# Weight conversion from 64-bit floats: two VectorE bit instructions and a product with zero in place of three VectorE instructions and a maximum

## The chip, the cores and the metric

The kernel runs on one core of a Trainium2 chip. The core has a matrix engine (TensorE, PE in the rows; PEld is its weight load), VectorE (DVE), ScalarE (ACT), GpSimd (POOL), SyncE (SP, which here only issues transfers) and 16 DMA engines. Each engine works through its own queue in order and waits for the others by semaphores. The metric is the device time of one execution, in microseconds; smaller is better.

## The reference

Three stages follow each other: attention inside chunks of 64 tokens, a channel mix with a squared ReLU and a sigmoid gate, and a top-2 mixture of four causal attention experts. What matters here is the second stage and the type of its weights:

```python
'w_k': np.random.randn(d_model, d_ff).astype(np.float32) * (1.0 / np.sqrt(d_model))
...
def _moe_ref(x, mu_k, mu_r, w_k, w_v, w_r) -> np.ndarray:
    x_prev = np.concatenate([np.zeros((B, 1, D), dtype=np.float32), x[:, :-1, :]], axis=1)
    xk = mu_k * x + (1.0 - mu_k) * x_prev
    xr = mu_r * x + (1.0 - mu_r) * x_prev
    k = np.maximum(xk @ w_k, 0.0)
    v = k * k @ w_v
    r = 1.0 / (1.0 + np.exp(-(xr @ w_r)))
    return (r * v).astype(np.float32)
```

The factor `1.0 / np.sqrt(...)` is a 64-bit float, so `w_k` (512 x 1024), `w_v` (1024 x 512) and `w_r` (512 x 512) arrive as 64-bit floats. The kernel reads them as pairs of 32-bit words and makes 32-bit floats of them itself.

## The kernel before, in words

`attn_mix` does the first two stages together. Tokens come in units of 384, twelve in all. For a unit, the attention steps (`s_T`, `s_S`, `s_PV`, `s_PT`) load queries, keys and values, transpose them on TensorE (line 148, result `Tps`), make scores (`Sps`, lines 182 and 185), a softmax on VectorE and ScalarE (lines 190 to 199) and the product with the values (`PVps`, lines 216 and 219), copied by ScalarE to `XT` (line 44). `s_shift` mixes each token with the one before it (lines 274 to 279, results `xhr`, `xlr`, `xhk`, `xlk`: a high and a low part each). Then come the products `mps` of the channel mix, on lines 57 to 59: three matmuls for each pair of blocks, high with high, low with high and high with low. So each weight is needed as a high part and a low part as well (`wrh`, `wrl`, `wkh`, `wkl`, `wvh`, `wvl`).

The weights are made by `conv` in 20 chunks of 128 x 512: 4 of `w_r`, 8 of `w_k`, 8 of `w_v`, in that order. A chunk's 512 KB are loaded into a tile `st` (line 340); `h` is every second word of it (sign, exponent and top of the mantissa), `l` the words between. ScalarE writes |h|, read as a 32-bit float, to the tile `cz` (line 346). POOL raises it to at least 2^-15 (line 347), so that a zero stays within the range that the bits can say. Three VectorE instructions then build the 32-bit float: shift left by 3 and mask (line 348), put in the top three bits of `l` (line 349), put in the sign of `h` (line 350). `split` makes the high part on POOL (line 46) and the low part on VectorE (line 360).

Two `st` buffers and two `cz` buffers go round (the first four chunks use other tiles for `st`). So the load of a chunk waits until line 350 of the chunk two before it is through; and it waits on SP's queue, ahead of the loads of queries, keys and values issued later.

Some 12 chunks are converted while the first attention tiles are made, by the order in `CFG["pro"]`; the others while the first unit's products run (`convert` in the last loop of `attn_mix`). In each engine's queue the instructions stand in an order that a planner made out of this program order, from its own idea of how long each takes; the trace shows attention and conversion interleaved one by one. After the twelve units come the experts, lines 485 to 901.

Of the kernel before, what the change touches and what calls it, by code (L numbers as in the profile page):

```python
# [11 lines left out]
ACTF = mybir.ActivationFunctionType  # L12
ALU = mybir.AluOpType
# [2 lines left out]
DRAM = bass.MemoryType.DRAM  # L16


F64_ZERO = 2.0 ** -15

CH = 64
UNIT = 384
# [26 lines left out]
def f32(ap):  # L49
    return ap.bitcast(F32)  # L50
# [11 lines left out]
def attn_mix(tc, at, x2T, q, k, v, mu_k, mu_r, w_k, w_v, w_r, ident, attended_all, mixed_k):  # L62

    nc = tc.nc
# [10 lines left out]
    scale = 1.0 / float(D) ** 0.5  # L75

    with ExitStack() as ctx:
# [254 lines left out]
        def conv(src, dst, g, c0, n):  # L332

            i = done[0] - 1
            if i < 4:

                st = wkr.tile([128, n, 2], I32, tag=("xhr", "xlr", "xhk", "xlk")[i], name="st")
            else:
                st = at.tile([128, n, 2], I32, tag="st", bufs=CFG["stb"], name="st")
            nc.sync.dma_start(out=st.rearrange("p f w -> p (f w)"),  # L340
                              in_=src.bitcast(I32)[g * 128:(g + 1) * 128, 2 * c0:2 * (c0 + n)])
            h, l = st[:, :, 1], st[:, :, 0]
            z = at.tile([128, n], F32, tag="cz", bufs=2, name="cz")
            b = z.bitcast(I32)

            nc.scalar.activation(out=z, in_=f32(h), func=ACTF.Abs)
            nc.gpsimd.tensor_scalar(z, z, F64_ZERO, None, op0=ALU.max)
            nc.vector.tensor_scalar(b, b, 3, 0x3FFFFFF8, op0=ALU.logical_shift_left, op1=ALU.bitwise_and)
            nc.vector.scalar_tensor_tensor(b, l, 29, b, op0=ALU.logical_shift_right, op1=ALU.bitwise_or)
            nc.vector.scalar_tensor_tensor(b, h, -(1 << 30), b, op0=ALU.bitwise_and, op1=ALU.bitwise_or)  # L350
            split(z, dst, g, c0, n)

        def conv32(src, dst, g, c0, n):
# [4 lines left out]
        def split(z, dst, g, c0, n):  # L358
            copy(nc, CFG["chi"], dst.hi[:, g, c0:c0 + n], z)
            eng(nc, nth(CFG["clo"], done[0])).tensor_tensor(dst.lo[:, g, c0:c0 + n], z, f32(dst.hi[:, g, c0:c0 + n]), op=ALU.subtract)  # L360
# [593 lines left out]
```

## Time and profile before

| | us |
|---|---|
| median of 3 runs | 1010.99 (1010.32 to 1011.34) |
| the profiled execution, its own time | 1009.65 |
| its span, first to last instruction | 1007.8 |
| PE busy | 950.1 (94%) |
| DVE busy | 682.0 (68%) |
| ACT busy | 547.2 (54%) |
| POOL busy | 396.4 (39%) |

The profiled execution took 1.34 us less than the median, and 1.85 us of it lie outside its span. Busy time is summed over the span; which engine limits a stretch is read from the busy time of that stretch and from the waits in it.

### The profile page before, as it was taken

Reading aid. Unit: us, or ns where it says so; the run is one execution under the profiler, and the core shown is the slowest. Engines: PE = TensorE matmul, PEld = TensorE weight load, DVE = VectorE, ACT = ScalarE, POOL = GpSimd, SP = SyncE. Lnnn points to the kernel's source line nnn. Section 1 sums busy time; section 2 is a strip of 40 time slices with the busy share of each in tenths; the row PEclk is TensorE's granted clock in tenths of the full one; section 3 lists DMA queues with packets and bytes.
Section 4 is the critical chain, followed back from the end, with each engine's and each line's share of the span. In section 5 each row is a group of like instructions: output and inputs, shape, how many; then the busy total and the mean of one; then the engine's idle time right before and its main releaser. Section 6 shows DMA issues by size and latency. Waiting matters only on the chain.

```text
span 1007.8 us, 21843 instructions
## 1 busy us (share of the span) xinstructions
PE 950.1 (94%) x8038; PEld 909.6 (90%) x8038; DVE 682.0 (68%) x1690; ACT 547.2 (54%) x1271; POOL 396.4 (39%) x519
## 2 busy tenths in 40 slices
PE   3679899998999999999999999999999999999997
PEld 2569899998999899999999999989899999989985
DVE  5899936557654766775667432587776867877895
ACT  3478564535343534444454413476666857676674
POOL 5444402636453645455454536413331232233101
PEclk8789999999999999999999999999999999999999
DMA  9784342253425352524223124674553547263412
GB/s 228 191 213 130 96 98 79 48 126 64 106 36 115 63 123 53 126 41 104 54 53 84 32 64 117 119 185 115 131 136 99 174 83 201 66 179 93 141 44 96
DMA packets 218979, 108.42 MB, mean 108 GB/s; under 512 B 182920, under 2 KB 195320, under 8 KB 218872
## 3 DMA queue, kind: packets, MB, share of 16 engines
q1 hardware_dynamic: 188600, 67.16, 29.2%
q0 software_dynamic: 30272, 39.86, 14.5%
q8 instruction: 64, 1.05, 0.5%
q14 instruction: 43, 0.35, 0.1%
HBM read 66.01 MB, written 28.38 MB: 94 GB/s over the span
## 4 chain that ended last, share of the span: by engine, by line
PE 53%; DVE 7%; ACT 2%; DMA 2%; issue 1%; POOL 0%; DVEq 0%; SPq 0%; ACTq 0%; POOLq 0%
PE mps L57 8%; PE mps L58 8%; PE mps L59 8%; PE pj L57 6%; PE pj L59 6%; PE pj L58 6%; PE Sps L657 4%; PE Tps L717 3%; PE AVps L750 2%; PE AVps L746 2%; DVE PTl L724 1%; DVE sm L659 1%; DMA x<-x2T 1%; ACT P L669 1%; DVE Q L554 1%
## 5 line engine op out<-in xcount | busy, mean ns | idle before, releaser
L57 PE MATMUL mps<-xhk,wkh 128*128 128x384 f32 x384 | 131.7, 344 | 4.6 <-DVE r L305 4.3
L58 PE MATMUL mps<-xlk,wkh 128*128 128x384 f32 x384 | 129.1, 337 | 0.0
L59 PE MATMUL mps<-xhk,wkl 128*128 128x384 f32 x384 | 128.9, 336 | 0.0
L57 PE MATMUL mps<-kh,wvh 128*128 128x384 f32 x384 | 128.0, 340 | 0.9 <-DVE r L305 0.9
L59 PE MATMUL mps<-kh,wvl 128*128 128x384 f32 x384 | 127.3, 335 | 0.9 <-DVE wvl L360 0.9
L58 PE MATMUL mps<-kl,wvh 128*128 128x384 f32 x384 | 128.0, 335 | 0.0
L309 POOL TENSOR_TENSOR kl<-r,kh 128x384 fp32r<-128x384 f32 x80 | 87.2, 1091 | 69.7 <-ACT kh L308 69.5
L305 DVE TENSOR_TENSOR r<-mps,r 128x384 f32<-128x384 f32 x80 | 44.4, 555 | 95.0 <-ACT r L302 83.3
L669 ACT ACTIVATE P<-sm,nm 128x512 f32<-128x512 f32 (+3 forms) x144 | 83.9, 584 | 24.0 <-DVE nm L659 19.9
L659 DVE CUSTOM_DVE_ANT_0 sm<-Sps,mask 128x256 f32<-128x256 f32 (+4 forms) x160 | 74.3, 477 | 22.4 <-PE Sps L657 21.2
L263 POOL TENSOR_TENSOR xa<-XT 128x384 f32<-128x384 f32 x72 | 67.6, 947 | 53.4 <-DVE xlr L279 27.6
L766 POOL TENSOR_TENSOR Yf<-Yf,zb 128x576 f32<-128x576 f32 x14 | 20.0, 1428 | 153.6 <-DVE Yf L761 153.3
L57 PEld LDWEIGHTS mps<-xhk,wkh 128*128 128x128 f32 x384 | 72.2, 188 | 6.9 <-DVE r L305 5.5
L308 ACT ACTIVATE kh<-r 128x384 fp32r<-128x384 f32 x96 | 50.7, 528 | 46.0 <-DVE r L305 45.1
L724 DVE TENSOR_TENSOR PTl<-Tps,PTh 128x512 fp32r<-128x512 f32 (+2 forms) x144 | 70.7, 504 | 6.9 <-ACT PTh L723 5.6
L57 PEld LDWEIGHTS mps<-kh,wvh 128*128 128x128 f32 x384 | 71.9, 188 | 1.9 <-DVE r L305 1.2
L59 PEld LDWEIGHTS mps<-kh,wvl 128*128 128x128 f32 x384 | 71.8, 188 | 1.2 <-DVE wvl L360 1.2
L58 PEld LDWEIGHTS mps<-xlk,wkh 128*128 128x128 f32 x384 | 72.3, 188 | 0.1
L59 PEld LDWEIGHTS mps<-xhk,wkl 128*128 128x128 f32 x384 | 72.2, 188 | 0.0
L58 PEld LDWEIGHTS mps<-kl,wvh 128*128 128x128 f32 x384 | 72.1, 188 | 0.1
L57 PE MATMUL mps<-xhr,wrh 128*128 128x384 f32 x192 | 66.5, 348 | 4.7 <-ACT sig L292 3.8
L277 DVE SCALAR_TENSOR_TENSOR xa<-xa,mu,XT 128x384 f32<-128x384 f32 x72 | 63.4, 893 | 10.8 <-POOL xa L263 10.8
(192 smaller groups left out, 2761.5 us busy)
## 6 DMA issues: line engine op xcount, KB each, us to landing
x2T<-x2d POOLq DMA_DIRECT2D x48, 384.0 KB, 3.4
x<-x2T POOLq DMA_DIRECT2D x32, 576.0 KB, 5.7
K<-Kph SPq DMA_DIRECT2D x64, 128.0 KB
out_dram<-o SPq DMA_DIRECT2D x32, 256.0 KB
ldq<-in_q_dram SPq DMA_DIRECT2D x176, 32.0 KB
ldk<-in_k_dram SPq DMA_DIRECT2D x176, 32.0 KB
ldv<-in_v_dram SPq DMA_DIRECT2D x20, 256.0 KB
st<-in_moe_w_k_dram SPq DMA_DIRECT2D x8, 512.0 KB
```

The lines of the kernel that those rows point to most:

```text
L57: nc.tensor.matmul(out=out, lhsT=ah, rhs=bh, start=first and i == 0, stop=False)
L58: nc.tensor.matmul(out=out, lhsT=ah, rhs=bl, start=False, stop=False)
L59: nc.tensor.matmul(out=out, lhsT=al, rhs=bh, start=False, stop=last and i == n - 1)
L263: nc.gpsimd.tensor_tensor(d, now, prev, op=ALU.subtract)
L277: nc.vector.scalar_tensor_tensor(a, d, m, prev, op0=ALU.mult, op1=ALU.add)
L305: nc.vector.tensor_tensor(r2, p, r, op=ALU.mult)
L308: nc.scalar.activation(out=o.hi, in_=r2, func=ACTF.Copy)
L309: eng(nc, CFG["klo"][u >= CFG["nearly"]]).tensor_tensor(o.lo, r2, f32(o.hi), op=ALU.subtract)
L657: issued = nc.tensor.matmul(out=pp[:, :w], lhsT=x, rhs=y[:, a:a + w], start=n == 0, stop=n == len(terms) - 1)
L659: nc.vector.tensor_tensor_reduce(out=sm[:, a:a + w], in0=pp[:, :w], in1=mk[:, :w], op0=ALU.add, op1=ALU.min, scale=-scale, scalar=3e38, ac ...
L669: nc.scalar.activation(out=x[:, :nk], in_=sm[:, :nk], func=ACTF.Exp, scale=-1.0, bias=nm[:, :1], accum_out=z)
L724: nc.vector.tensor_tensor(l, src, f32(h), op=ALU.subtract)
```

## The change

ScalarE no longer writes |h| but h times 2^-112, sign and all, which takes the difference of the two exponent offsets away. POOL no longer works on `cz`: it multiplies h by zero in place, in the tile `st`, at every second word, and what stays of h is its sign bit alone. VectorE joins the top three bits of `l` with that sign, in place of `l`, also at every second word of `st`; and a second VectorE instruction shifts `cz` left by 3 and joins it with `l`. The shift pushes the sign of `cz` out, so no mask is needed. What comes after (`split`) is as before.

```diff
-F64_ZERO = 2.0 ** -15
+F64_BIAS = 2.0 ** -112
...
-            nc.scalar.activation(out=z, in_=f32(h), func=ACTF.Abs)
-            nc.gpsimd.tensor_scalar(z, z, F64_ZERO, None, op0=ALU.max)
-            nc.vector.tensor_scalar(b, b, 3, 0x3FFFFFF8, op0=ALU.logical_shift_left, op1=ALU.bitwise_and)
-            nc.vector.scalar_tensor_tensor(b, l, 29, b, op0=ALU.logical_shift_right, op1=ALU.bitwise_or)
-            nc.vector.scalar_tensor_tensor(b, h, -(1 << 30), b, op0=ALU.bitwise_and, op1=ALU.bitwise_or)
+            nc.scalar.activation(out=z, in_=f32(h), func=ACTF.Copy, scale=F64_BIAS)
+            nc.gpsimd.tensor_scalar(f32(h), f32(h), 0.0, None, op0=ALU.mult)
+            nc.vector.scalar_tensor_tensor(l, l, 29, h, op0=ALU.logical_shift_right, op1=ALU.bitwise_or)
+            nc.vector.scalar_tensor_tensor(b, b, 3, l, op0=ALU.logical_shift_left, op1=ALU.bitwise_or)
```

## Rows read from the trace of the kernel before

**Rows 1.** Page, part 2: busy tenths of 40 slices of 25.2 us, and granted clock

```profile
PE   3679899998999999999999999999999999999997
PEclk8789999999999999999999999999999999999999
```

**Rows 2.** Busy us by stretch: start:end, length, engines, clock, DMA share, GB/s

```profile
0.00:62.00 62.00, 31.55 (x536) 25.01 (x536) 45.45 (x73) 28.21 (x51) 30.02 (x36) 0.79 0.86 212
62.00:120.00 58.00, 51.79 (x508) 49.24 (x507) 55.29 (x93) 43.67 (x87) 24.42 (x20) 0.96 0.52 136
120.00:525.00 405.00, 398.30 (x3724) 388.94 (x3725) 248.73 (x408) 188.08 (x359) 191.00 (x219) 1.00 0.39 81
560.00:1008.00 448.00, 433.64 (x3030) 412.24 (x3028) 310.76 (x1079) 272.79 (x740) 134.97 (x225) 1.00 0.44 115
```

**Rows 3.** Waits of PE, 62 to 120 us: total us, times, longest

```profile
PE mps L57 <- ACT sig L292: 3.3, 1, 3.3
PE Sps L185 <- ACT kT L150: 1.6, 1, 1.6
PE mps L59 <- DVE wvl L360: 0.9, 1, 0.9
```

**Rows 4.** Waits of SP's queue, first 62 us, then 62 to 120 us

```profile
SPq L340 <- DVE cz L350: 9.4, 3, 5.3
...
SPq L340 <- DVE cz L350: 13.9, 7, 6.3
```

**Rows 5.** Conversion lines: ns min/median/max, starts; then groups with busy us, mean ns

```profile
L347 POOL TENSOR_SCALAR cz<-cz x20: 1473/1488/2412, 5.0 to 109.6; 128x512 f32<-128x512 f32 x20
L348 DVE TENSOR_SCALAR cz<-cz x20: 411/422/830, 6.5 to 112.0; 128x512 int32<-128x512 int32 x20
L349 DVE SCALAR_TENSOR_TENSOR cz<-st,cz x20: 631/691/978, 7.4 to 113.3; 128x512 int32<-128x512 int32 x20
...
L46 POOL CAST wkh<-cz 128x512 fp32r<-128x512 f32 x8 | 5.3, 668 | 13.9 <-DVE cz L350 13.9
...
L274 ACT ACTIVATE xb<-XT,mu 128x384 f32<-128x384 f32 x16 | 9.9, 625 | 1.7 <-DVE xlk L279 1.0 <-DVE xlr L279 0.6
L346 ACT ACTIVATE cz<-st 128x512 f32<-128x512 f32 x20 | 13.6, 679 | 17.5 <-DMA st<-in_moe_w_k_dram 11.4 <-DMA st<-in_moe_w_r_dram 4.1 <-DVE wkl L360 1.5
```

**Rows 6.** Timeline of VectorE, one chunk: start us, us, what, [idle before]

```profile
24.05 0.43 DVE L348 TENSOR_SCALAR cz<-cz 128x512 int32<-128x512 int32 x1 [0.38 <-POOL cz L347]
24.51 0.69 DVE L349 SCALAR_TENSOR_TENSOR cz<-st,cz 128x512 int32<-128x512 int32 x1
```

**Rows 7.** Timeline of all engines, steps on the way to the first mix product

```profile
27.88 0.80 DVE L348 TENSOR_SCALAR cz<-cz 128x512 int32<-128x512 int32 x1 [0.32 <-POOL cz L347]
28.60 1.21 DVE L199 TENSOR_TENSOR P<-P,m 128x1024 f32<-128x1024 f32 x1
...
34.40 0.43 DVE L348 TENSOR_SCALAR cz<-cz 128x512 int32<-128x512 int32 x1 [1.38 <-POOL cz L347]
...
49.81 0.43 DVE L348 TENSOR_SCALAR cz<-cz 128x512 int32<-128x512 int32 x1 [0.28 <-POOL cz L347]
50.15 0.68 DVE L191 TENSOR_TENSOR P<-Sps,m 128x512 f32<-128x512 f32 x1
...
51.47 0.69 DVE L350 SCALAR_TENSOR_TENSOR cz<-st,cz 128x512 int32<-128x512 int32 x1
...
52.30 1.77 SPq L340 DMA_DIRECT2D st<-in_moe_w_k_dram  x1
...
54.34 0.66 ACT L346 ACTIVATE cz<-st 128x512 f32<-128x512 f32 x1 [1.92 <-DMA st<-in_moe_w_k_dram]
...
57.63 2.67 PE L185 MATMUL Sps<-kT,qT 64*64 64x64 f32 x64 [0.83 <-ACT kT L150]
...
62.23 0.69 PE L57 MATMUL mps<-xhr,wrh 128*128 128x384 f32 x1
```

**Rows 8.** Timeline of ScalarE late in the conversion

```profile
111.55 0.52 ACT L278 ACTIVATE xhk<-xb 128x384 fp32r<-128x384 f32 x1 [1.56 <-DVE xb L275]
```

## The prediction

> **What bounds the kernel now.** I read the page's slices first, to see where TensorE is not full [rows 1]. Its busy share is low in the first three slices only, and its granted clock is below full there too; from about 120 us on it is nearly always busy. The table by stretch says it in microseconds [rows 2]: from 120 to 525 us TensorE is busy 398.30 of 405.00, from 560 to 1008 us 433.64 of 448.00, but in the first 62 us only 31.55, and from 62 to 120 us 51.79 of 58.00. All 20 chunks of the conversion start between 5.0 and 109.6 us on POOL [rows 5], so the change lies wholly in the two stretches where TensorE has idle time: 30.4 us in the first, 6.2 us in the second. What the first 120 us lose or win moves all the rest with it, one for one, since TensorE sets the pace behind them.
>
> In the first stretch the DMA engines have a share of 0.86 and VectorE 45.45 of 62 us; in the second the DMA share is 0.52 and VectorE has 55.29 of 58 us, with TensorE 51.79 [rows 2]. So the first stretch is a chain of loads and short steps, and in the second VectorE's queue is as full as TensorE's. The waits show how the conversion gets into both. SP waited for line 350, the last bit instruction of a chunk, for 9.4 us in three waits in the first stretch and 13.9 us in seven in the second [rows 4], since that instruction gives `st` back; loads of queries, keys and values queue behind. And in the second stretch TensorE waited 3.3 us for ScalarE's sigmoid, 1.6 us for `kT` and 0.9 us for `wvl` [rows 3].
>
> **The change part by part.**
>
> *VectorE, three instructions to two.* The one that goes is line 348, 422 ns in the median [rows 5]. What it takes from the queue is less or more than that by what follows. Line 349 needs its result and starts 0.46 us behind it, at 24.51 after 24.05 [rows 6]; where an unrelated instruction follows, the step is 0.34 us, 50.15 after 49.81 [rows 7]. So a chunk gives VectorE 0.34 to 0.46 us back, 20 chunks 6.8 to 9.2 us. The two that stay have the type and size of lines 349 and 350: 691 ns [rows 5]. The first now also writes at every second word. No VectorE row writes so; lines 349 and 350 read so, at 691 ns, and line 349 has its longest at 978 ns [rows 5]. I take 691 ns, because reading at that step costs no more than the median says; the upper end, 0.29 us more, would take most of the gain away. An instruction that runs shorter than 691 ns is not excluded either, with 631 ns as the shortest [rows 5].
>
> *ScalarE, Abs to Copy with a scale.* Same tile, same reading at every second word: line 346 has a mean of 679 ns [rows 5]. Line 274 is a Copy with a scale, 625 ns for 384 elements [rows 5]. I take no difference; the ends are what these two rows span, some 0.05 us less, or 0.15 us more if the scale costs line 274's price for each of 512 elements (625 x 512/384 = 833 ns). ScalarE is busy 43.67 of 58 us in the second stretch [rows 2], and that is the cover.
>
> *POOL, a maximum in `cz` to a product in `st`.* This is the unknown of the change. It is still one instruction of the tensor-scalar type on 512 elements, which took 1488 ns in the median [rows 5], but it multiplies, and it reads and writes at every second word. Nearest below is POOL's cast of the same size, 668 ns [rows 5]; nearest above the longest of line 347 itself, 2412 ns [rows 5]. I take 1488 ns, since that row has the same type, size and immediate operand. It remains on the chain of a chunk: it must let ScalarE read h before it overwrites it, so it still waits for ScalarE, and VectorE's first instruction still waits for it. No wait is added or dropped and no engine is freed of one. `st` is given back by the last VectorE instruction as before, now the second.
>
> [...]
>
> *What of it lies on the path.* Followed back from the first mix product at 62.23 us [rows 7]: TensorE comes to it after the scores at 57.63, which waited for `kT` from ScalarE; ScalarE's queue had stood still for 1.92 us until the weights landed at 54.34; their load was issued at 52.30, right after line 350 (51.47 to 52.16) gave the buffer back; that chunk's line 348 is at 49.81. Its own weights waited on SP behind loads that queue behind the chunk with line 348 at 34.40; that one started once ScalarE had the transposed probabilities made from line 199 at 28.60, which stood behind line 348 at 27.88. So three chunks of the twelve lie on the path. They give 0.72 us (28.60 after 27.88, a slow one), 0.46 and 0.34 us: 1.5 us together. At the low end the loads hide it, since the DMA share is 0.86, and the gain is 0; at the high end all twelve chunks are on the path with 0.46 us each, 5.5 us.
>
> From 62 to 120 us VectorE is nearly full, and eight chunks times 0.34 us are 2.7 us that it gets back. TensorE can take of that only where its wait goes back to VectorE: the 0.9 us for `wvl`, and the 1.6 us for `kT`, which stood in ScalarE's queue behind an instruction that had waited 1.56 us for VectorE's `xb` at 111.55 [rows 3, 8]. That is 2.5 us; the 3.3 us for the sigmoid are ScalarE's queue, and I count nothing of them. What is late next in both waits is ScalarE's own work, 43.67 of 58 us, so I take 2.0 of the 2.5 us.
>
> *The sum.* 1.5 + 2.0 = 3.5 us. The profiled execution of 1009.65 us would come to 1006.15 us; against the median, which is 1.34 us above it, 1010.99 - 3.5 = 1007.5 us, with 0 to 5.5 + 2.7 = 8.2 us as the bounds of the VectorE part.
>
> **The rivals.**
>
> *Hidden by the loads.* The first stretch is set by the DMA engines and SP's order of issue, and in the second the waits go to ScalarE instead. For it: the DMA share of 0.86, and line 346 idle 15.5 us for its loads (11.4 and 4.1, [rows 5]). Against it: SP's own waits for line 350 [rows 4]. Then the gain is the 0.9 us of `wvl` or less: 1010.1 us, within the bound of no change.
>
> *POOL's product is slower, and the kernel with it.* The mechanism is the in-place product at every second word. A chunk's chain is ScalarE, POOL, VectorE: it loses as soon as POOL takes more than 0.46 us longer than 1488 ns, that is from 1.95 us on. At 2412 ns it is 0.92 - 0.46 = 0.46 us longer for each chunk; with three chunks on the first path and eight in the second stretch, 11 x 0.46 = 5 us, 1016 us. For it: no row shows POOL writing like this. Against it: POOL is busy 30.02 of 62 us and 24.42 of 58 us [rows 2], so its queue has room. [...]
>
> *POOL's product is faster.* At the cast's 668 ns a chunk's chain shortens by a further 0.82 us; on the three chunks of the path that is 2.5 us more, 1005.0 us.
>
> *The planner's order shifts.* The queues are ordered by a planner that goes by its own durations, and one VectorE instruction less in 20 places lets it put attention and conversion together differently. TensorE's idle time behind 120 us is 6.7 us and 14.4 us in the two stretches [rows 2], most of it in short waits; a new order moves some of these to either side. I count 3 us to either side, from about a seventh of those 21 us: 1004.5 or 1010.5 us with the forecast's gain, and up to 1014 us with none of it.
>
> **How the numbers follow.** The forecast (gain of 2 to 5.5 us) has 0.40, the faster POOL 0.10, the hidden gain 0.20, the slower POOL 0.10, the planner 0.20, of which 0.07 ends faster, 0.03 the same and 0.10 slower. A measurement of this kernel can tell from no change about 0.2%, 2.0 us: faster is below 1009.0 us, slower above 1013.0 us. Faster: 0.40 + 0.10 + 0.07 = 0.57. The same: 0.20 + 0.03 = 0.23. Slower: 0.10 + 0.10 = 0.20. The range that leaves out one in ten at each end reaches below to the whole VectorE part, 8.2 us, with a little of a faster POOL, 1001.5 us; above to the planner's loss with half of the slower POOL's, 1014.0 us. The forecast's own range is 1005.5 to 1009.0 us.
>
> **What would show it right or wrong.** The VectorE group of line 348 is gone and the two left have medians near 690 ns; if the first has 0.9 us or more, the gain is eaten there. POOL's product has a median of about 1.49 us; near 0.7 or above 1.95 us a POOL rival holds. The first mix product starts at about 60.7 us instead of 62.23; if it starts at 62 us, the loads hid it. SP's waits for the last bit instruction are smaller in total than 9.4 and 13.9 us. The waits of TensorE for `kT` and `wvl` before 120 us shrink to half a microsecond together. If all of this holds and the time does not move, TensorE's idle time behind 120 us has grown, and it was the planner. The prediction would be wrong most plainly if the conversion's queue order in the first 60 us is another one, because then the path of three chunks is not the path any more.

## The result, and the profile after

The kernel became slower: 1017.52 us (median of six, 1015.78 to 1018.49) against 1010.47 us of before beside it, a ratio of 1.0063 with a 95% interval of 1.0052 to 1.0074. The prediction was 1007.5 us, with a range up to 1014.0 us; sign and range were both wrong. The profiled execution took 1016.21 us, with a span of 1014.4 us.

Each operation costs what the prediction said. Lines of the conversion in the trace of after (least, median and longest ns, first and last start; the numbering of after, where 348 and 349 are the two bit instructions that are left), answering to [rows 5]:

```profile
L346 ACT ACTIVATE cz<-st x20: 657/669/717, 4.2 to 96.7; 128x512 f32<-128x512 f32 x20
...
L347 POOL TENSOR_SCALAR st<-st x20: 1529/1580/2145, 4.9 to 97.4; 128x512 f32<-128x512 f32 x20
...
L348 DVE SCALAR_TENSOR_TENSOR st<-st x20: 620/690/1112, 6.5 to 100.2; 128x512 int32<-128x512 int32 x20
...
L349 DVE SCALAR_TENSOR_TENSOR cz<-cz,st x20: 677/692/1133, 7.7 to 101.4; 128x512 int32<-128x512 int32 x20
```

The bit instructions are at 690 and 692 ns (691 predicted, the write at every second word costs nothing), POOL's product is at 1580 ns (1488 predicted, far under the 1.95 us from which it would lose). But the last chunk starts at 97.4 us on POOL, not at 109.6: the conversion now runs earlier, ahead of other work.

The busy time by stretch of after (as [rows 2]) shows where TensorE lost time:

```profile
0.00:62.00 62.00, 28.65 (x400) 22.45 (x400) 40.89 (x59) 26.24 (x46) 33.16 (x37) 0.70 0.83 212
62.00:120.00 58.00, 53.21 (x488) 51.32 (x489) 50.12 (x83) 40.51 (x79) 26.72 (x24) 0.91 0.46 124
120.00:525.00 405.00, 395.99 (x3823) 386.43 (x3822) 253.10 (x405) 192.56 (x362) 183.11 (x210) 0.99 0.40 83
560.00:1008.00 448.00, 438.47 (x3064) 418.00 (x3063) 312.69 (x1084) 273.59 (x743) 137.28 (x229) 1.00 0.44 115
```

Up to 62 us TensorE is busy 28.65 us instead of 31.55, and the granted clock is 0.70 instead of 0.79, then 0.91 instead of 0.96. (The clock of the first stretch says little: it is 0.90 in the kernel `new_seam_335` below, whose order is that of after up to 330 us.) From 120 to 525 us, where no conversion is left, TensorE is busy 395.99 instead of 398.30 us. So time goes in two places, and one of them is far behind the change.

Waits of TensorE from 62 to 120 us (as [rows 3]):

```profile
PE mps L57 <- ACT sig L292: 4.0, 1, 4.0
PE Tps L148 <- DVE P L199: 2.9, 1, 2.9
```

Waits of SP's queue for the last bit instruction, first 62 us, then 62 to 120 us (as [rows 4]):

```profile
SPq L340 <- DVE cz L349: 12.1, 4, 4.9
...
SPq L340 <- DVE cz L349: 25.6, 6, 6.4
```

The waits for `kT` and `wvl` are gone, as the forecast wanted, but others have come. SP waits 12.1 and 25.6 us for the last bit instruction instead of 9.4 and 13.9, though a chunk has one VectorE instruction less: that can't be the instructions, it is where they stand. The two traces say so, compared instruction by instruction in each queue (by line, operation and tile, without the buffer numbers, and with line 348 of before left out): at least 206 of 1510 places on VectorE's queue hold another instruction than before, 171 of 1104 on ScalarE's, 66 of 519 on POOL's, 62 of 708 on SP's and 1084 of the 8038 matmuls. They lie in patches, each with the same instructions in another sequence; most up to 165 us, others out to 525 us, where the change touched nothing.

### The profile page after: what moved, and what is told of

The parts are those of the page before. It is cut to its first block, busy times and chain, and to the rows that moved or that the text cites. A ratio compares the mean times of both kernels' runs of the same rounds, so it can differ in the third digit from the quotient of the medians.

```text
span 1014.4 us, 21855 instructions
## 1 busy us (share of the span) xinstructions
PE 953.5 (94%) x8038; PEld 914.0 (90%) x8038; DVE 679.8 (67%) x1670; ACT 551.3 (54%) x1271; POOL 399.9 (39%) x519
## 4 chain that ended last, share of the span: by engine, by line
PE 75%; DVE 11%; ACT 4%; DMA 3%; issue 3%; POOL 2%; SPq 2%; DVEq 0%; ACTq 0%; POOLq 0%
PE mps L57 15%; PE mps L59 14%; PE mps L58 14%; PE pj L57 6%; PE pj L59 6%; PE pj L58 5%; PE Sps L656 4%; PE Tps L716 3%; PE Tps L148 2%; PE AVps L749 2%; PE AVps L745 2%; DVE PTl L723 1%; DVE sm L658 1%; DMA st<-in_moe_w_k_dram 1%; ACT P L194 1%
## 5 line engine op out<-in xcount | busy, mean ns | idle before, releaser
L277 DVE SCALAR_TENSOR_TENSOR xa<-xa,mu,XT 128x384 f32<-128x384 f32 x72 | 63.8, 900 | 12.4 <-POOL xa L263 12.4
```

Source lines behind the costliest of these rows:

```text
L277: nc.vector.scalar_tensor_tensor(a, d, m, prev, op0=ALU.mult, op1=ALU.add)
```

## The experiments

All kernels are timed beside before on the same chip; a time is a median, the interval is that of the ratio to before. To hold an order, the program is built twice: first with one conversion body, from which the order of each queue is read, then with the body that runs, each queue chained into that order by `NoSync` edges, meant to order the issue alone:

```diff
+        for a, b in pairs:
+            tc.add_manual_dep(by_name[b], a, mybir.DependencyInfo(mybir.DependencyClass.NoSync, mybir.DependencyReason.DATA), reason="pin")
```

Lines 345 to 351 keep the numbers of before in all these kernels; with the new body the two bit instructions are 348 and 349.

### Operations or order

The new operations in the order of before (`new_in_old`). The edit: the five lines of `conv` as in the change, and the order read from the body of before.

> The new conversion (Copy with a scale, product with zero on POOL, two VectorE instructions), with all five queues (TensorE, VectorE, ScalarE, POOL, SP) held in the order that they have in the kernel before; the place of the removed instruction simply falls away. Theory A (the planner's new order is the whole loss, the operations are as cheap as priced): the removed instruction gives back what the prediction said, 1005 to 1009 us, and the first mix product comes before 62.2 us. Theory B (the new operations cost the time themselves, for instance the dependent step of 0.80 us between the two bit instructions or the product in place on POOL): about 1016 to 1018 us in the old order too. Theory C (the operations are neutral, hidden by the loads, and only the order costs): 1009 to 1012 us.

Measured: 1008.21 us against 1010.38, ratio 0.9981 (0.9971 to 0.9990). The first mix product starts at 61.61 us. Waits of TensorE from 62 to 120 us in that run (`issue` is time in which it waited for nothing that the profile shows):

```profile
PE mps L57 <- ACT sig L292: 2.7, 1, 2.7
PE Tps L148 <- issue: 1.3, 1, 1.3
PE Sps L185 <- ACT kT L150: 0.9, 1, 0.9
PE mps L59 <- DVE wvl L360: 0.6, 1, 0.6
```

The operations alone make the kernel 2.2 us faster by the medians (1.0 to 2.9 us by the ratio's interval). 1.6 us of it is seen in three waits, each shorter than in [rows 3]: 3.3 to 2.7, 1.6 to 0.9, 0.9 to 0.6 us. Two kernels below that have the same order up to 165 us (`new_order_late_only`, `new_in_old_seam_245`) show the three within 0.1 us of these.

The converse, the operations of before in the order of the changed kernel (`old_in_new`).

> The conversion of before (three VectorE instructions), with all five queues held in the order that the changed kernel has; the extra instruction stands right ahead of the next of its chunk. Theory A (the order is the loss): as slow as the changed kernel or slower by what twenty more VectorE instructions cost in that order, 1017 to 1022 us. Theory B (the new operations cost the time): as fast as before, 1009 to 1012 us.

Measured: 1022.30 us, ratio 1.0120 (1.0106 to 1.0134), just above the range of Theory A; the third instruction costs some 5 us in this order. Theory B is out from both sides; the order is the loss. It costs 9.3 us by the medians (1017.52 less 1008.21), 8.3 us by the ratios.

The removed instruction alone (`old_two_in_old`):

```diff
             nc.scalar.activation(out=z, in_=f32(h), func=ACTF.Abs)
             nc.gpsimd.tensor_scalar(z, z, F64_ZERO, None, op0=ALU.max)
-            nc.vector.tensor_scalar(b, b, 3, 0x3FFFFFF8, op0=ALU.logical_shift_left, op1=ALU.bitwise_and)
             nc.vector.scalar_tensor_tensor(b, l, 29, b, op0=ALU.logical_shift_right, op1=ALU.bitwise_or)
```

> The kernel before without the first bit instruction of a chunk (line 348; the shift and the mask are left out of the weights), all else as before, in the order of before. It prices the removed instruction alone, without the Copy, the product in place and the write at every second word. Theory A: 1005.5 to 1009 us, as the prediction's forecast of 3.5 us; if the loads hide it (the first rival), 1010 us. What the new conversion in the old order has above this is the price of its operations (0.09 us on POOL and a later write, expected 0 to 1 us together).

Measured: 1008.28 us, ratio 0.9978 (0.9968 to 0.9987). This kernel leaves out the shift and the mask, so its weights are wrong numbers. The time is that of `new_in_old` to 0.1 us, so the Copy with a scale, the product in place and the write at every second word together cost nothing that can be measured here, where either ratio is known to about 1 us to each side.

The same operations in the order that the planner makes of them itself (`old_two_own`).

> The kernel before without line 348 (the shift and the mask are left out of the weights), in the order that the planner itself makes of that, which is neither the order of before nor that of the changed kernel. In the order of before the same operations took 1008.3 us. If the planner's order moves the time whatever the operations (Theory A): somewhere from 1006 to 1020 us, off 1008.3 by more than 1 us. If only the changed kernel's own operations (the product in place, its waits) lead the planner astray: 1007.5 to 1009 us.

Measured: 1010.49 us against 1010.52, ratio 0.9999 (0.9986 to 1.0012). The planner's order takes the whole 2.2 us away here too. So it isn't the change's own operations that lead it astray; one VectorE instruction less in 20 places is enough to move the order, and the amount it costs differs (2.2 and 9.3 us).

### Where the order costs

The order of before up to about 120 us, the planner free behind that (`new_early_old`).

> The new conversion; each queue holds the order of before only up to about 120 us (the first 692 TensorE, 145 VectorE, 134 ScalarE, 54 POOL and 100 SP instructions), and what stands behind that is in the order that the planner of the changed program gives it. If the changed kernel's loss in the first 120 us (about 3.5 us by its progress) and the one at 335 us (another 3.5 us) are separate, this keeps only the second, if the planner makes the same choice there: 1009 to 1013 us. If the whole loss is made in the first 120 us and the later one follows from it: as all five queues in the old order, 1005 to 1009 us. If neither order matters (Theory B): 1016 to 1018 us.

Measured: 1017.67 us, ratio 1.0079 (1.0063 to 1.0094). With the early part mended the time is as bad as the changed kernel's. The number lies in the range of the third expectation, that neither order matters, but `new_in_old` has ruled that out; the other two missed. Left to itself the planner made a third order behind 120 us; its trace has TensorE waits of 2.30 us at 121.87, 4.78 us at 247.47 and 2.49 us at 495.58 us where before has none above 1.5 us. So a part must be held, not left free, to be priced. Both parts were then held (`new_order_early_only`: the changed kernel's order up to about 165 us, that of before behind; `new_order_late_only`: the other way round).

> The new conversion; the queues hold the changed kernel's order in the part in which conversion and attention share the queues (about the first 165 us), and the order of before behind it. Theory A1 (the order costs in separate places, and the costs add up): the lag at 140 us was 3.1 us in the changed kernel against 2.7 us of lead with the old order, so some 5.8 us of the 9.3 us that lie between them: 1013 to 1015 us. Rival A2 (what is late early on is taken up by waits later, so that only the late order counts): 1007 to 1010 us. Rival A3 (only the whole order does it, one part brings it all): 1016 to 1018 us.

> The counterpart: the new conversion; the order of before in the first 165 us, and the changed kernel's order behind it. Theory A1: 9.3 us less the 5.8 us of the early part, 3.5 to 4.5 us on top of 1008.2 us: 1011.5 to 1013 us. Rival A2: 1016 to 1018 us. Rival A3: 1008 or 1017 us, nothing between.

Measured: 1013.26 us, ratio 1.0026 (1.0016 to 1.0037), and 1012.52 us, ratio 1.0020 (1.0011 to 1.0030), against 1010.58. Above `new_in_old` that is 5.0 and 4.3 us, together 9.3 us: the costs add up, A1. Rivals A2 and A3 are out. The traces show the late part by itself. From the 1301st matmul of a trace (at about 165 us) to the 4721st (at about 520 us) every kernel does the same matmuls; TensorE needs 357.9 and 357.0 us for them in the order of before (`new_in_old`, `new_order_early_only`) and 362.0 and 360.7 us in the changed one (after, `new_order_late_only`).

### The late part: one place at 335 us

Timeline of after there, VectorE, then ScalarE, then TensorE:

```profile
334.21 1.22 DVE L196 TENSOR_REDUCE m<-P 128x16 f32<-128x1024 f32 x1 [1.13 <-ACT P L194]
...
336.14 1.49 DVE L277 SCALAR_TENSOR_TENSOR xa<-xa,mu,XT 128x384 f32<-128x384 f32 x2
337.69 2.11 DVE L279 TENSOR_TENSOR xlr<-xa,xhr 128x384 fp32r<-128x384 f32 x1
339.72 0.54 DVE L305 TENSOR_TENSOR r<-mps,r 128x384 f32<-128x384 f32 x1
...
333.12 1.06 ACT L194 ACTIVATE P<-P 128x1024 f32<-128x1024 f32 x1 [2.94 <-DVE P L191]
334.08 1.19 ACT L44 ACTIVATE XT<-PVps 128x256 f32<-128x256 f32 x4
...
340.32 0.69 PE L57 MATMUL mps<-xhk,wkh 128*128 128x384 f32 x1 [4.71 <-DVE r L305]
```

ScalarE waits 2.94 us for the softmax with four ready copies (line 44) behind the exponential; so the token shift that reads them (277, 279) comes late on VectorE, and line 305, which reads a finished `mps` and so gives TensorE its place back for the next one, stands behind it. Before had the copies ahead of the exponential, and a shorter wait of TensorE:

```profile
326.65 1.22 ACT L44 ACTIVATE XT<-PVps 128x256 f32<-128x256 f32 x4 [0.34 <-PE PVps L216]
...
330.55 1.06 ACT L194 ACTIVATE P<-P 128x1024 f32<-128x1024 f32 x1 [1.39 <-DVE P L191]
...
334.47 0.44 PE L57 MATMUL mps<-xhk,wkh 128*128 128x384 f32 x1 [1.42 <-DVE r L305]
```

The edit (`new_seam_335`) restores 12 positions on VectorE, the first eight of which are shown, 5 on ScalarE and 7 on POOL:

```diff
 ScalarE
-L194, L44, L44, L44, L44
+L44, L44, L44, L44, L194
 VectorE
-L196, L197, L198, L277, L277, L279, L305, L279
+L277, L196, L277, L279, L197, L305, L198, L279
```

> The changed kernel in its own order but for one place at about 335 us, where TensorE stood 4.71 us for line 305: there 12 instructions of VectorE, 5 of ScalarE and 7 of POOL stand again as in the kernel before (the copies of line 44 ahead of the exponential of line 194, lines 277, 279 and 305 ahead of lines 196 to 198). Theory A1: TensorE's wait there shrinks from 4.71 to about 1.4 us, and the granted clock doesn't fall behind it (it was 0.74 from 340 to 350 us, which is 2.6 us more): 1017.5 less 3.3 to 5.0, 1012.5 to 1014.5 us. Rival (the lag comes back at the next place, or the wait has another cause): 1016.5 to 1018 us.

Measured: 1014.19 us, ratio 1.0035 (1.0021 to 1.0049). TensorE in that run:

```profile
339.93 0.44 PE L57 MATMUL mps<-xhk,wkh 128*128 128x384 f32 x1 [1.41 <-DVE r L305]
```

and its busy time and clock from 330 to 350 us, first of after, then of `new_seam_335` (length, PE, PEld, DVE, ACT, POOL, clock, DMA share, GB/s):

```profile
330.00:340.00 10.00, 5.61 (x33) 5.29 (x31) 8.74 (x13) 3.65 (x9) 4.43 (x5) 0.92 0.54 99
340.00:350.00 10.00, 9.68 (x44) 9.55 (x45) 7.24 (x10) 5.17 (x12) 7.94 (x8) 0.74 0.38 59
```

```profile
330.00:340.00 10.00, 8.59 (x166) 8.20 (x165) 8.73 (x17) 5.98 (x12) 3.33 (x5) 1.00 0.44 85
340.00:350.00 10.00, 9.44 (x52) 8.59 (x53) 7.21 (x9) 3.95 (x9) 8.22 (x8) 1.00 0.41 63
```

The wait is 1.41 us instead of 4.71, and the granted clock behind it, from 340 to 350 us, is 1.00 instead of 0.74. 3.3 us of the late 4.3 us are this one place (2.8 us by the ratios). What the clock cost beside the wait can be bounded. From the 2901st to the 3501st matmul, the same work in both, after needs 67.86 us (328.52 to 396.38 us) and `new_seam_335` 64.71 us (331.43 to 396.14 us): TensorE is idle 4.71 against 2.55 us there and busy 63.15 against 62.16 us. So 2.2 of these 3.15 us are idle time, and slower matmuls account for some 1.0 us at most, not for the 2.6 us that the expectation reckoned from ten microseconds at 0.74.

The other direction, one patch of the changed kernel's order put into the good order (`new_in_old_seam_245`).

> The new conversion in the order of before, but for one place at about 240 to 265 us, where the changed kernel's order was the better one (before and the new conversion in the old order have TensorE waits of 1.48 and 1.07 us there, the changed kernel none): there VectorE, ScalarE, POOL and TensorE stand as in the changed kernel. Theory A1 (the costs of single places add up, whichever order they are from): 1008.2 less 2.2 to 2.6: 1005.5 to 1006.5 us, the fastest of all. Rival (a place's order suits only what stands ahead of it): 1008 us or more.

Measured: 1008.33 us, ratio 0.9974 (0.9966 to 0.9983), no gain over `new_in_old`. The two waits, 1.48 and 1.06 us at 238 and 242 us in `new_in_old`, have become one of 0.41 us, but the wait for the sigmoid behind them, 0.50 us in `new_in_old`, is 1.53 us there. From the 2101st to the 2501st matmul the trace gains 0.7 us (51.55 against 52.21 us), less than the medians can show. That removed waits add up held for the two halves and for 335 us, and not here: the rival.

### The early part: waits that move

The order ahead of 62 us or behind it (`new_order_to_62`)?

> The new conversion; the queues hold the changed kernel's order up to what had started at 62 us (295 TensorE, 59 VectorE, 45 ScalarE, 33 POOL and 59 SP instructions), and the order of before behind that. Theory A1 (the early loss is made by the order ahead of 62 us): all of the 5.0 us, 1012.5 to 1014.5 us. Rival (it is the order behind 62 us, where products and attention are interleaved in another way): 1008 to 1010 us.

Measured: 1012.46 us against 1010.66, ratio 1.0026 (1.0016 to 1.0035): 4.3 of the 5.0 us are made by the order ahead of 62 us (by the ratios, all of them). Timeline of after there, ScalarE, VectorE, TensorE:

```profile
53.15 0.66 ACT L346 ACTIVATE cz<-st 128x512 f32<-128x512 f32 x1 [5.07 <-DMA st<-in_moe_w_k_dram]
55.59 0.72 ACT L346 ACTIVATE cz<-st 128x512 f32<-128x512 f32 x1 [1.78 <-DMA st<-in_moe_w_k_dram]
56.21 0.57 ACT L150 ACTIVATE PT<-Tps 128x512 f32<-128x512 f32 x1
...
49.75 1.06 DVE L348 SCALAR_TENSOR_TENSOR st<-st 128x512 int32<-128x512 int32 x1 [3.91 <-POOL st L347]
...
52.13 1.28 DVE L190 TENSOR_REDUCE m<-Sps 128x8 f32<-128x512 f32 x2
...
54.10 1.08 PE L148 MATMUL Tps<-ident,ldq 128*128 128x128 f32 x4 [5.23 <-issue]
```

The conversion stands ahead of ready attention work: VectorE waits 3.91 us with a softmax behind it, ScalarE 5.07 us with the copy of line 150 behind it. That looked like the cause. Four edits put the attention first, step by step (in the diff below, the minus lines are the order of after, the plus lines the new one; `new_place_50`: VectorE's lines 190, 191 and ScalarE's 150, 194; `new_two_places`: with the place at 335 us; `new_place_50b`: lines 196 to 199 and 274 as well; `new_two_places_b`: with 335 us):

```diff
 ScalarE (new_place_50)
-L346, L346, L346, L150, L194, L150, L150
+L346, L150, L194, L150, L150, L346, L346
 VectorE (new_place_50b)
-L348, L349, L360, L190, L190, L191, L360, L191, L348, L349, L196, L348, L197, L349, L198, L360, L199
+L190, L190, L191, L191, L348, L349, L360, L360, L196, L197, L198, L199, L348, L349, L348, L349, L360
```

> The changed kernel in its own order but for one place at about 50 us: VectorE does the softmax lines 190 and 191 of the next tile ahead of the bit instructions of the chunk (there they waited behind line 348, which waited 3.91 us for POOL), and ScalarE does the copy of the transposed probabilities (line 150), the exponential (line 194) and two more copies of line 150 ahead of two line 346 that wait for their loads. Theory A1 (the early loss is this one place): TensorE's wait of 5.2 us at 54.10 us goes, most of the 5.0 us of the early order come back: 1012.5 to 1014 us. Rival (the loads of SP, held up behind a load of weights that waits for line 349, set the pace there whatever the order on VectorE and ScalarE): 1016 to 1018 us.

> The changed kernel in its own order with both places mended, the one at 50 us and the one at 335 us. Theory A1: the gains add up, 3.3 us of the second (measured) and 4 to 5 us of the first: 1009 to 1010.5 us, so level with before or a little faster. Rival (the first place gives nothing): 1014 us.

> The changed kernel in its own order but for the place at 48 to 62 us, now mended to its end: on VectorE the whole softmax of the tile (lines 190, 191, 196 to 199) stands ahead of the bit instructions of the second and third chunk, on ScalarE the copies and the exponential of that tile and line 274 ahead of the third chunk. Theory A1 (three chunks ahead of one softmax are the early loss): the wait of 11.26 us at 63.7 us shrinks to a few us, 1012.5 to 1014.5 us. Rival (the loads of queries, keys and values that stand behind two weight loads on SP's queue set the pace): 1016 to 1018.5 us.

> As the one before, with the place at 335 us mended too. Theory A1: the gains add up, 1009 to 1011 us, level with before. Rival: 1013 to 1015 us, as with the first half of the mending.

Measured: 1018.02 us (1.0065 to 1.0090), 1014.02 us (1.0027 to 1.0052), 1017.61 us (1.0062 to 1.0088) and 1013.94 us (1.0019 to 1.0044), in the order of the expectations. The place at 335 us gave its part again; the place at 50 us gave nothing, in any of the four. Waits of TensorE from 45 to 90 us, in turn after, `new_place_50` and `new_place_50b`:

```profile
PE Tps L148 <- issue: 5.2, 1, 5.2
PE mps L57 <- ACT sig L292: 4.0, 1, 4.0
PE Tps L148 <- DVE P L199: 2.9, 1, 2.9
```

```profile
PE Tps L148 <- DVE P L199: 11.3, 1, 11.3
PE mps L57 <- ACT sig L292: 4.5, 1, 4.5
PE Tps L148 <- issue: 1.9, 1, 1.9
```

```profile
PE mps L57 <- ACT sig L292: 4.8, 1, 4.8
PE Tps L148 <- DVE P L199: 4.4, 1, 4.4
PE PVps L219 <- ACT PT L150: 3.0, 1, 3.0
```

The wait at 54 us is gone, and in `new_place_50b` TensorE comes to its 405th matmul at 58.11 instead of 63.62 us; but it waits somewhere else then, and at 80 us 541 matmuls have started instead of 542. The last wait left is for the sigmoid, behind an exponential on ScalarE; two more kernels take that away (`new_sig` alone, `new_three_places` with 50 and 335 us):

```diff
 ScalarE at 71 to 82 us
-L278, L278, L274, L346, L194, L274, L278, L292, L346, L278, L292, L292, L292
+L278, L292, L278, L274, L292, L346, L274, L292, L278, L292, L194, L346, L278
```

> The changed kernel in its own order, but at 71 to 82 us ScalarE does the four sigmoids of line 292 ahead of the exponential of line 194 (which then stands behind them), and VectorE does line 196 of that tile behind lines 275, 279 and 348. Theory S (the early loss is paid at the sigmoid): TensorE's wait of 4.05 us at 79 us goes, 1013.5 to 1015 us. Rival B (VectorE's backlog from the stall at 46 to 50 us sets the pace, TensorE only waits elsewhere then): 1016.5 to 1018.5 us.

> The changed kernel in its own order with all three places mended: the softmax ahead of the conversion at 48 to 62 us, the sigmoids ahead of the exponential at 71 to 82 us, and the place at 335 us. With 50 and 335 us alone it took 1013.9 us. Theory S: 4 us less, 1009 to 1010.5 us, level with before. Rival B: 1013 to 1014.5 us.

Measured: 1017.51 us against 1010.83, ratio 1.0066 (1.0052 to 1.0079), and 1014.42 us, ratio 1.0033 (1.0021 to 1.0045): nothing again, as Rival B said for both. Waits from 45 to 90 us in `new_three_places`, then in `new_in_old`:

```profile
PE Tps L148 <- DVE P L199: 5.7, 1, 5.7
PE PVps L219 <- ACT PT L150: 2.9, 1, 2.9
PE mps L57 <- ACT xhk L278: 2.8, 2, 2.1
PE Tps L148 <- ACT kT L150: 1.8, 1, 1.8
```

```profile
PE Tps L148 <- DVE P L199: 3.2, 2, 2.1
PE mps L57 <- ACT sig L292: 2.7, 1, 2.7
PE Tps L148 <- issue: 1.3, 1, 1.3
```

Summed over all rows of that view TensorE waits 12.7 us in after, 18.3, 13.7, 15.4 and 15.1 us in `new_place_50`, `new_place_50b`, `new_sig` and `new_three_places`, and 8.1 us in `new_in_old`. These sums are of one trace each and can't rank the mended kernels: in `new_order_early_only` and `new_seam_335`, whose order is that of after up to 165 us, the sum is 15.8 and 17.9 us.

A longer count separates idle and busy time. Up to the 1301st matmul all these kernels have done the same matmuls. TensorE, in us:

| order ahead of 165 us | traces | reaches it at | idle | busy |
|---|---|---|---|---|
| of before (`new_in_old`, `new_in_old_seam_245`, `new_order_late_only`) | 3 | 158.3 to 161.7 | 34.2 to 35.7 | 124.1 to 126.1 |
| changed (after, `new_order_early_only`, `new_seam_335`) | 3 | 164.7 to 168.3 | 38.1 to 41.4 | 126.1 to 126.9 |
| changed and mended (the six with the places at 50 or 71 us) | 6 | 166.4 to 167.8 | 37.3 to 45.0 | 122.7 to 129.0 |

So the early loss is idle time in the main. The granted clock from 62 to 80 us is 0.77 to 0.85 in the three traces of the changed order (0.78 in after) and 0.82 to 1.00 in the three of before (1.00 in `new_in_old`); the busy time in the table is a microsecond or so longer in the changed order, and the mended kernels are no better than the unmended ones.

From 62 to 80 us VectorE is busy 17.4 to 17.8 of 18 us in all the kernels of the sums, the good order too. The orders differ in how many chunks stand ahead of the first unit's shift in VectorE's queue: ahead of the first step of line 275 the bit instructions of 12 chunks in after, where that step starts at 62.52 us, and of 10 in before and in `new_in_old`, where it starts at 56.63 and 56.65 us. All mended kernels kept the 12; the planner's own order of `old_two_own`, which cost only 2.2 us, has 10. This fits Rival B, that conversion ahead of the first unit's shift is a backlog which no move of single instructions behind it pays back. It is not shown, for no run here moved those two chunks behind the shift. Another candidate stays open beside it: SP issues two weight loads in a row at 47.45 us and stands 4.56 us with the loads of values and queries behind them. SP's order alone was not tried.

### What one VectorE instruction costs

One more for each chunk (`old_four_in_old`) and one less again (`old_one_in_old`), both in the order of before:

```diff
 old_four_in_old
-            nc.vector.tensor_scalar(b, b, 3, 0x3FFFFFF8, op0=ALU.logical_shift_left, op1=ALU.bitwise_and)
+for by in (3, 0): extra(nc.vector.tensor_scalar(b, b, by, 0x3FFFFFF8, op0=ALU.logical_shift_left, op1=ALU.bitwise_and))
 old_one_in_old
-            nc.vector.tensor_scalar(b, b, 3, 0x3FFFFFF8, op0=ALU.logical_shift_left, op1=ALU.bitwise_and)
-            nc.vector.scalar_tensor_tensor(b, l, 29, b, op0=ALU.logical_shift_right, op1=ALU.bitwise_or)
```

> The kernel before in its own order, with one more bit instruction for each chunk (line 348 a second time, with a shift of zero). It prices one VectorE instruction of that size on the path from the other side. If the price is as the instruction that was taken away gave it (2.1 us for twenty chunks): 1012.5 us. If the prediction's 0.34 to 0.46 us hold for eleven chunks: 1013.5 to 1015.5 us. If the loads hide it: 1010.5 us.

> The kernel before with only the last of the three bit instructions (lines 348 and 349 are left out, and so the shift, the mask and the low word of the weights), in the order of before. Line 349 took 691 ns where line 348 took 422 ns. If VectorE still sets the path: twice as much or more as the 2.1 us that line 348 gave, 1003 to 1006 us. If the path then goes over the loads and ScalarE (the first rival of the prediction, in part): little more, 1007 to 1008.5 us.

Measured: 1016.48 us against 1010.52, ratio 1.0065 (1.0051 to 1.0079), above all three expectations, and 1004.12 us against 1010.66, ratio 0.9935 (0.9922 to 0.9948), as the first expectation had it. (`old_one_in_old` leaves out the low words too, so its weights are wrong numbers as well.) In one order the kernel goes 1016.5, 1010.5, 1008.3, 1004.1 us with four, three, two and one bit instruction: 6.0, 2.1 and 4.2 us a step. VectorE is on the path throughout, so the loads don't hide it; but a step is worth 0.30, 0.11 and 0.21 us a chunk (each over 20). The last step takes away 691 ns and the other two 422 ns each [rows 5], and yet these two differ by a factor of almost three; no row of before tells them apart.

## Why the prediction was wrong, and where it was right

**Costs of the operations: right.** VectorE 691 ns predicted, 690 and 692 measured; ScalarE no difference predicted, a mean of 673 ns against 679; POOL 1488 predicted, 1580 measured. All of them together are priced by `new_in_old` against `old_two_in_old`: 0.1 us. The rivals of a slower and of a faster POOL are out: the product, which reads and writes at every second word, takes 92 ns more than the 1488 ns of the maximum, a different operation.

**The sum of 3.5 us: mechanism right, size too large.** In the order of before it is 2.2 us. The term "1.5 us before the first mix product" did not show: that product starts at 61.61, 63.63 and 62.56 us in `new_in_old`, `old_two_in_old` and `old_one_in_old`, against 62.23 us [rows 7]. One trace can't show such a term: in `new_order_late_only` and `new_in_old_seam_245`, which are the same as `new_in_old` up to there, that product starts at 63.8 and 63.7 us. Of the term "2.0 of the 2.5 us" for `kT` and `wvl` 1.0 us came (0.7 and 0.3), and 0.6 us for the sigmoid, of which nothing was counted. The likely reason, not shown, is that the path of three chunks, followed back in one trace, was one path among several of nearly the same length; taking 0.34 to 0.72 us off it leaves the next one.

**Hidden by the loads: out.** `old_one_in_old` gains 4.2 us over `old_two_in_old`, and `old_four_in_old` loses 6.0 us against before.

**The planner's order shifts: this was the case, and its price was the step that failed.** The forecast's sum of 3.5 us has no term for the order; the rival beside it had a chance of 0.20 and "3 us to either side", worked out from a seventh of TensorE's idle time behind 120 us. The new order cost 9.3 us, 5.0 of it ahead of 165 us and 4.3 behind. The 3 us were too small because they shared out idle time that was there in before; a new order makes new idle time, 4.71 us at one place where before has 1.42, with a granted clock of 0.74 behind it, from 340 to 350 us (1.00 in before from 335 to 345 us). It left out the first 120 us, where attention and conversion are interleaved and more than half of the loss came. And it took either side as equally likely: of the planner's own two orders without line 348, one costs 2.2 us and one 9.3 us against the order of before. Two don't make a rule, but neither gained.

**What would show it right or wrong.** VectorE's two medians came as said, and POOL's nearly. That the waits for `kT` and `wvl` went was luck: the new order took them away and put others in their place, and in the order of before they are 0.9 and 0.6 us, three times the half microsecond that was said. The first mix product came at 68.39 instead of 60.7 us, and SP's waits grew. The text named "the conversion's queue order in the first 60 us is another one" as what would make it wrong most plainly, and that is what happened; it gave no chance of its own to it.

**A version that beats both** is `new_in_old`: the change with the order of before kept, 1008.21 us, 0.2% under before and 0.9% under the change as it stands.

## What to carry to other kernels

Where a planner orders the queues, an edit of instructions is also an edit of the order, far beyond the place of the edit: compare the order of the queues before reading any wait, hold the old order to price the operations, and price the order by itself, part by part with every part held. Don't bound a reordering by the idle time of the old trace. Before two traces are compared over a stretch, see how far two traces of one order lie apart there: the sum from 45 to 90 us was 12.7 to 17.9 us in three. A wait that is long in the new trace is not yet the loss: seven kernels here mended waits of 4 to 5 us; the one place where TensorE had no other wait near by gave its time back, the crowded stretch gave none.

## What the runs showed of the hardware that was not expected

Taking away a 422 ns instruction of VectorE made the next one slower. Groups of the bit instructions from 0 to 120 us (busy us and mean ns), first in before, then in `old_two_in_old`, where line 348 is the instruction that is line 349 in before:

```profile
L349 DVE SCALAR_TENSOR_TENSOR cz<-st,cz 128x512 int32<-128x512 int32 x20 | 14.0, 698 | 0.3
...
L348 DVE TENSOR_SCALAR cz<-cz 128x512 int32<-128x512 int32 x20 | 9.6, 479 | 12.1 <-POOL cz L347 12.1
```

```profile
L348 DVE SCALAR_TENSOR_TENSOR cz<-st,cz 128x512 int32<-128x512 int32 x20 | 16.1, 804 | 14.2 <-POOL cz L347 14.2
```

The same instruction has a mean of 804 ns instead of 698 once it is the first behind POOL: 2.1 us of the 9.6 us of VectorE time are given back at once. Six of its 20 take 1.07 to 1.10 us, and each of the six starts while an instruction of POOL is running (line 46 or 347); two others start so, beside lines 253 and 347, and take 0.68 us. In before one of the 20 of line 349 takes over 0.9 us; there it was line 348 that stood first behind POOL, and three of its 20 took 0.80 to 0.83 us. In after six of the 20 of line 348 take 1.06 to 1.11 us, each of them begun while an instruction of POOL is running (line 46 or 347); four others begin so, beside the same lines, and take 0.62 to 0.72 us. So the long ones are found beside a running POOL, though not each time, and the time added doesn't go with how long POOL still runs (POOL's spans are rough): at 49.75 us in after VectorE takes 0.37 us more than its median beside a cast that goes on for 0.51 us, and at 6.52 us 0.42 us more beside a product that goes on for 1.47 us. What makes VectorE take longer there, the traces don't show.
